# The last product of a two-MLP kernel: from part Strassen to Strassen for all k pairs, with tiles parked in DRAM

## Chip, core and metric

The kernel runs on one core of a Trainium2 chip. Its time is the device time of one execution in microseconds: a median of 524.71 us over three runs (524.4 to 524.81). Traces come from a further execution taken with the hardware profiler. TensorE (PE) multiplies matrices out of SBUF into PSUM; VectorE (DVE) and ScalarE (ACT) work element by element; SP only issues DMAs here. Each engine works off its own instructions in order and waits for the others at semaphores.

## What is computed

Attention with a sigmoid in place of the softmax (2 batches, 12 heads, 448 positions, 64 per head); then two MLPs on the 896 tokens of 768 features:

```python
scores = scale * q @ k.T - log(448)
x = sigmoid(scores) @ v                          # 896 x 768
xn = x / rms(x) * g
x = (silu(xn @ w_gate) * (xn @ w_val)) @ w_out   # 768 -> 1536 -> 768
h = x @ w_in                                     # 768 -> 2048
out = (h * sigmoid(h)) @ w_out2                  # 2048 -> 768
```

All data is float32. The change is in the very last product, of K = 2048 (16 k tiles of 128, so 8 k pairs) with an output of 768 x 896, which is three chunks of two 128-row tiles by two batches of 448 columns.

## The kernel before

**Products.** A float32 operand is split into a high part rounded to fp32r and a low part, the rest (`high` on ScalarE, `low` on VectorE). A product of two tiles is three matmuls of 448 columns (`PASSES`: high-high, high-low, low-high). Activations stay in SBUF with features on partitions; weights come from DRAM in slabs of up to six 128x128 tiles, in an integer form that ScalarE (`exponent`, `tail_act`) and VectorE (`merge`) turn into float32. The pieces that matmuls read, high and low of up to 384 columns, lie in a ring of nine (`RING`); slabs arrive in two buffers (`raw`).

**Strassen.** A pair of k tiles, a pair of output tiles and the two batches form a 2x2 block product. Plainly (`weight_std`, `product`) that is eight tile products. `weight_mac` and `group` do it in seven, in Winograd's form: weights A11, A12, A22 and the sums S1 to S4 (four VectorE operations more), activations B11, B21, B22 and T1 to T4. `ORDER_OF` is the order of the seven groups; one group runs over all k pairs in turn. What must be added between the results is saved from PSUM by ScalarE (`save`) and added by VectorE; TensorE adds further products into the same bank once that bank is saved.

**Activations for Strassen.** `formed` makes all seven from a float32 tile of a k pair (on VectorE seven operations of 448 columns and two of 896, on ScalarE three and two) and needs 3.5 tiles of [128, 2, 2, 448]; `halved` only splits (2 tiles); `late` makes the T's of a halved pair with the 640-column tile `spare` as its only room (14 VectorE and 4 ScalarE operations of 448 columns). The input product's outputs g2_0 to g2_7 are such float32 tiles. There are 23.5 tiles in all: `whole` lists free ones, `part` free halves, `reserve` how many wholes others must leave.

**The last product before.** Chunk 0 (e0) takes k pairs 0 to 3 by Strassen and 4 to 7 plainly, chunk 1 (e1) 0 to 4 and 5 to 7, both by `mixed` with the plain part first. Chunk 2 (e2, `phased`) takes pairs 0 to 2 by Strassen, pair 7 plainly, then pairs 3 to 6. Pairs 0 and 1 are formed during the input product; 2 and 3 when its last tile has begun; 4 to 7 are halved, and `late` turns 4, 5 and 6.

**Order.** `Plan` holds all this work as jobs with costs and dependencies. Matmuls have a fixed order; `Plan.run` gives each job of VectorE (D), ScalarE (A) and SP (S) a due time counted back from its users and places it by list scheduling over fixed costs (`LAG`, line 37: a DMA takes 0.4 us of SP and lands 4.4 us later). The instructions are issued in the order so found. SP issues all weight loads (line 237) and all output stores (line 1382).

Of the kernel before, what the change touches and what calls it, by code (L numbers as in the profile page):

```python
# [34 lines left out]
IDLE = 9  # L35
SQUARED = 10
# [15 lines left out]
RESERVE = 6  # L52
# [143 lines left out]
def tile_attention_two_mlps(  # L196
# [378 lines left out]
    ep = ctx.enter_context(tc.tile_pool(name="ep", bufs=1, reuse_waits="tile"))  # L575
    pools = {"T": tp, "F": fp, "x": xp, "r": rp, "e": ep}
# [16 lines left out]
    whole, part, reserve = [], {}, [0]  # L593
# [178 lines left out]
    ORDER_OF = ("A11", "S1", "S2", "A12", "S3", "S4", "A22")  # L772
    USES = dict(zip(ORDER_OF, ("B11", "T1", "T2", "B21", "T3", "B22", "T4")))

# [175 lines left out]
    def phased(name, phases, slab, keys, book, fdep, put, own):  # L950
# [3 lines left out]
        single = {a: Banks(f"{name}{a}") for a in ("A11", "S1", "S2", "S3")}  # L954
        where = dict(single, A12=ba.bank(0), S4=ba.bank(1), A22=bb.bank(0))
        bw = bb.bank(1)
        opens = dict(single, A12=ba, A22=bb)
        saved, e = {}, {}
# [8 lines left out]
        def add(j, src, other, deps):  # L967
            def go():
                if j not in saved:
                    saved[j] = saved_tile(name, j)  # L970
                tt(saved[j], src(), saved[other], ALU.add)

            return dve(S, go, deps)

        def save(j, src, dep):
            def go():
                saved[j] = saved_tile(name, j)
                nc.scalar.activation(saved[j], src(), AF.Copy)

            return scalar(S, go, [dep, sdone[j]], psum=True)  # L980

        list(groups(0))
        w = [6 * slab + i for i in range(2 * len(keys))]
        n = len(keys)
        product([where["A12"], where["S4"]], w[:n], keys, (0, 1), first=False, final=False)
        product([where["A22"], bw], w[n:], keys, (1,), last=False)
        p2 = product([where["A22"], bw], w[n:], keys, (0,), first=False, final=False)
        w1 = save(3, bw, p2[-1])
        for n in range(1, len(phases) - 1):
            list(groups(n))  # L990
        for a, g in groups(len(phases) - 1):
            if a == "A11":
                v0 = save(0, where[a], g)
                single[a].read_by(v0)
            elif a == "S1":
                v1 = save(1, where[a], g)
                single[a].read_by(v1)
# [67 lines left out]
    def late(key, q, deps, free, book, fdep, own):  # L1065

        (h11, l11), (h12, l12), (h21, l21), (h22, l22) = [
            [lambda m=m, j=j, b=b: act[key, 2 * q + m](j, b) for j in range(2)] for m in range(2) for b in range(2)
        ]
        t = spare[:, :S]  # L1070
        last = list(deps)

        def op(a, b, what, **more):
            get = lambda v: t if v is None else v().bitcast(F32)
            last[:] = [dve(S, lambda: tt(t, get(a), get(b), what), list(last), **more)]
            return last[0]

        def parted(name, to=None, deps=()):
            def hi_():
                if to:  # L1080
                    book[name] = tuple(v() for v in to)
                else:
                    h = half(f"{key}{q}{name}")
                    book[name] = (h[1][:, 0], h[1][:, 1])
                    own[name] = [h]
                high(book[name][0], t)

            h = scalar(S, hi_, last + list(deps), need=None if to else some)
            last[:] = [dve(S, lambda: low(book[name][1], t, book[name][0]), [h])]
            fdep[name] = list(last)  # L1090

        def plain_ones():
            for name, p in (("B11", (h11, l11)), ("B21", (h21, l21)), ("B22", (h22, l22))):
                book[name] = tuple(v() for v in p)

        begin = op(h12, h11, ALU.subtract, take="alt")
        begin.then(plain_ones)
        for name in ("B11", "B21", "B22"):
            fdep[name] = [begin]
        op(None, l12, ALU.add)  # L1100
        op(None, l11, ALU.subtract)
        parted("T1")
        op(h22, None, ALU.subtract)
        op(None, l22, ALU.add)
        parted("T2")
        op(None, h11, ALU.subtract)
        op(None, l11, ALU.subtract)
        parted("T3")
        op(h21, lambda: book["T2"][0], ALU.subtract)
        op(None, lambda: book["T2"][1], ALU.subtract)  # L1110
        op(None, l21, ALU.add)
        parted("T4", (h12, l12), [free])
        plan.frees("alt", last[0])

    def formed(key, q, tile_, deps, book, fdep, own, gate=None):
# [27 lines left out]
        ls = split(f"{key}{q}t", srcs, [[t1, t3], [t2, t4]], keep, lambda: tile_.back(int(q < 2)))  # L1143
# [20 lines left out]
    class Whole:  # L1164
# [96 lines left out]
    for p in range(1, NP1):  # L1261
# [7 lines left out]
        if p in (1, 2):  # L1269
            formed("h", p - 1, f[p - 1], fdone[p - 1], hbook[p - 1], hdep[p - 1], hown[p - 1])  # L1270
# [63 lines left out]
    def over():  # L1334
        give_all(hrest)
        reserve[0] = RESERVE

# [5 lines left out]
    gbook, gdep, gown, grest = [{} for q in range(5)], [{} for q in range(5)], [{} for q in range(4)], []  # L1343
# [156 lines left out]
```

## Time and profile before

| | us |
|---|---|
| median of three timed runs | 524.71 |
| span of the profiled execution | 527.0 |
| TensorE busy | 522.6 |
| VectorE busy | 467.4 |
| ScalarE busy | 378.3 |
| DMA, mean over the span | 122 GB/s |

The page gives no time of the profiled execution beside its span, first to last instruction. A busy time is what an engine spent in instructions. Matmuls are pipelined and overlap in the trace, so their number and the distance of their starts say more than the length of one.

### The profile page before, as it was taken

The numbers are of one execution on the slowest core, as the hardware profiler recorded it, in microseconds if no ns is written. First come the engines' busy times: TensorE is split into PE (matmuls) and PEld (weight loads), VectorE is DVE, ScalarE is ACT, GpSimd is POOL, SyncE is SP. The second block draws the span as 40 slices with busy tenths as digits, with TensorE's granted clock in tenths as the row PEclk, the third lists the DMA queues.
The fourth block names the chain that finished last, engine by engine and source line by source line (L and its number), as shares of the span: only waits on it lengthen the run. The fifth ranks groups of instructions, "written<-read, shape, count | busy, mean of one in ns | idle before, by whom it ended". The sixth has DMA issues, their size and how long they took to land.

```text
span 527.0 us, 7412 instructions
## 1 busy us (share of the span) xinstructions
PE 522.6 (99%) x2678; PEld 447.4 (85%) x2678; DVE 467.4 (89%) x855; ACT 378.3 (72%) x658; POOL 0.2 (0%) x4
## 2 busy tenths in 40 slices
PE   9999999999999999999999999999999999999997
PEld 4444469999999999999999999999899999999996
DVE  6799999999998979799989899998875999969984
ACT  6876754787877686857596688998887967565540
POOL 0000000000000000000000000000000000000000
PEclk9999999999999999999999999999999999999999
DMA  8764111033333343412533543422533214525201
GB/s 303 284 247 159 60 61 60 1 120 121 119 121 119 125 176 92 150 40 66 194 109 111 168 153 115 163 95 101 176 111 121 99 61 133 171 95 187 75 1 70
DMA packets 16292, 65.01 MB, mean 123 GB/s; under 512 B 2048, under 2 KB 4608, under 8 KB 16256
## 3 DMA queue, kind: packets, MB, share of 16 engines
q1 hardware_dynamic: 16112, 64.32, 35.4%
q8 instruction: 21, 0.34, 0.3%
q10 hardware_dynamic: 144, 0.23, 0.1%
q14 instruction: 15, 0.12, 0.1%
HBM read 61.79 MB, written 2.75 MB: 122 GB/s over the span
## 4 chain that ended last, share of the span: by engine, by line
PE 98%; DVE 1%; ACT 1%; issue 0%; ACTq 0%
PE sc L380 6%; PE av L407 6%; PE v L737 3%; PE e2S L786 2%; PE e1x L786 2%; PE g L737 2%; PE e0x L786 2%; PE e0b L737 2%; PE e0a L737 2%; PE o2x L786 2%; PE o1x L786 2%; PE o0x L786 2%; PE e2a L786 2%; PE i5x L786 1%; PE i4x L786 1%; PE e1b L737 1%
## 5 line engine op out<-in xcount | busy, mean ns | idle before, releaser
L267 DVE SCALAR_TENSOR_TENSOR f<-f,raw 128x768 uint32<-128x768 uint32 (+1 forms) x68 | 61.6, 907 | 9.1 <-ACT f L255 7.3
L263 ACT ACTIVATE raw<-raw 128x768 int32<-128x768 uint32 (+1 forms) x68 | 56.9, 841 | 15.8 <-DMA raw<-in_w 12.2
L255 ACT ACTIVATE f<-raw 128x768 f32<-128x768 f32 (+1 forms) x68 | 58.5, 862 | 7.2 <-DVE w_S L246 3.2
L243 ACT ACTIVATE w_S<-f 128x384 fp32r<-128x384 f32 (+1 forms) x82 | 40.8, 500 | 18.1 <-DVE f L695 6.4
L246 DVE TENSOR_TENSOR w_S<-f,w_S 128x384 fp32r<-128x384 f32 (+1 forms) x82 | 43.4, 531 | 8.4 <-ACT w_S L243 7.6
L389 ACT ACTIVATE a<-sc,logs 128x896 f32<-128x896 f32 x42 | 39.2, 1008 | 15.5 <-PE sc L380 15.5
L243 ACT ACTIVATE w_A<-f 128x384 fp32r<-128x384 f32 (+2 forms) x79 | 39.1, 503 | 12.6 <-PE o2y L737 1.8
L246 DVE TENSOR_TENSOR w_A<-f,w_A 128x384 fp32r<-128x384 f32 (+2 forms) x79 | 41.5, 536 | 4.8 <-ACT w_A L243 4.5
L407 PE MATMUL av<-a,vr 128*64 128x448 f32 (+1 forms) x192 | 35.4, 552 | 0.0
L407 PEld LDWEIGHTS av<-a,vr 128*64 128x64 f32 (+1 forms) x192 | 10.4, 135 | 21.3 <-issue 20.3
L380 PEld LDWEIGHTS sc<-ks 64*128 64x128 f32 x204 | 18.5, 188 | 10.7 <-issue 5.0
L380 PE MATMUL sc<-ks 64*128 64x448 f32 x204 | 25.2, 385 | 0.0
L246 DVE TENSOR_TENSOR w<-f,w 128x384 fp32r<-128x384 f32 (+1 forms) x34 | 15.7, 482 | 3.8 <-ACT w L243 3.6
L243 ACT ACTIVATE w<-f 128x384 fp32r<-128x384 f32 (+1 forms) x34 | 15.3, 464 | 5.2 <-PE o0x L786 1.1
L243 ACT ACTIVATE w_S<-s 128x384 fp32r<-128x384 f32 x24 | 12.5, 520 | 6.4 <-PE g L737 3.1
L737 PE MATMUL v<-x,w 128*128 128x448 f32 x72 | 15.3, 370 | 0.0
L737 PE MATMUL g<-x,w 128*128 128x448 f32 x72 | 15.3, 368 | 0.0
L737 PEld LDWEIGHTS g<-x,w 128*128 128x128 f32 x72 | 13.4, 188 | 1.7 <-issue 0.7
L737 PEld LDWEIGHTS v<-x,w 128*128 128x128 f32 x72 | 13.5, 188 | 1.4 <-issue 0.4
L702 DVE TENSOR_TENSOR f<-f 128x384 f32<-128x384 f32 (+2 forms) x27 | 14.3, 532 | 0.2
L246 DVE TENSOR_TENSOR w_S<-s,w_S 128x384 fp32r<-128x384 f32 x24 | 13.2, 552 | 0.9 <-ACT w_S L243 0.9
L246 DVE TENSOR_TENSOR ks<-kq,ks 128x896 fp32r<-128x896 f32 (+2 forms) x14 | 13.2, 949 | 0.4
(1461 smaller groups left out, 1489.0 us busy)
## 6 DMA issues: line engine op xcount, KB each, us to landing
raw<-in_w SPq DMA_DIRECT2D x56, 768.0 KB, 4.4
raw<-in_w SPq DMA_DIRECT2D x18, 512.0 KB, 3.6
kq<-in_kq SPq DMA_DIRECT2D x11, 448.0 KB, 5.4
vr<-in_v SPq DMA_DIRECT2D x6, 256.0 KB, 5.0
vr<-in_v SPq DMA_DIRECT2D x6, 192.0 KB, 2.5
out_t<-e0s SPq DMA_DIRECT2D x4, 224.0 KB, 3.0
out_t<-e1s SPq DMA_DIRECT2D x4, 224.0 KB, 2.2
out_t<-e2s SPq DMA_DIRECT2D x4, 224.0 KB, 1.9
```

The costliest lines, as they stand in the source:

```text
L243: nc.scalar.activation(dst, src, AF.Copy)
L246: nc.vector.tensor_tensor(dst, src, hi.bitcast(F32), ALU.subtract)
L255: nc.scalar.activation(floats[s], words(s)[:, :, 1].bitcast(F32), AF.Prelu, scale=2.0**-112, alpha=2.0**32)
L263: nc.scalar.activation(z.bitcast(I32), z, AF.Copy, scale=2.0**-29 * (1 - 2.0**-18), bias=-0.5 + 2.9e-5)
L267: nc.vector.scalar_tensor_tensor(fu, fu, 3, words(s)[:, :, 0], ALU.logical_shift_left, ALU.bitwise_or)
L380: nc.tensor.matmul(ps[to, h, :S], k_[:, keys], q_, start=(step == 0), stop=(step == 2 or plain), skip_group_check=True,)
L389: nc.scalar.activation(a, ps[:, :, :S], AF.Sigmoid, bias=logs, scale=D**-0.5)
L407: nc.tensor.matmul(av[n][h * D : (h + 1) * D, :S], vr[i][rows, c, h, :], a[rows, h, :], start=(begun[n] == 1), stop=(begun[n] == KC + 1), ...
L702: s4 = dve(hw, lambda: tt(block(1), block(1), block(0), ALU.subtract), [s2, l3])
L737: nc.tensor.matmul(banks[b](), t[:, jw], act[key](jx, b), start=(first and i == 0 and n_ == 0), stop=(final and i == n - 1 and n_ == 2), s ...
L786: nc.tensor.matmul(ps(), w[:, jw, j * P : (j + 1) * P], book[t][USES[a]][jx], start=(start and i == 0 and n == 0), stop=(stop and i == len ...
```

## The change

All eight k pairs of all three chunks go by Strassen.

Pairs 0, 1 and 2 are formed during the input product (`FIRST`). g2_3 to g2_6 are written to DRAM when they are done and brought back when a tile is free and the pair named in `AFTER` is through (`away`); then each is formed, as is pair 7. `halved` and `late` are no longer used for the last product.

Chunk 0 runs as e0 (pairs 0 to 3) and e0b (4 to 7), chunk 1 as e1 (0 to 4) and e1b (5 to 7). The first part (`half_sum` without `put`) leaves its sum in a float32 tile, which goes to DRAM; the second part (with `put`) gets it back, adds every result onto it, seven VectorE additions in place of three saves and three additions, and stores the output. The order is e0, e1, e2, e0b, e1b. Chunk 2 takes four phases of two pairs, its sums kept in PSUM, and gives back the tiles of each pair as it goes. Its weights come in slabs of four tiles. All new DMAs are issued by SP.

Cut to its core; left out are the deletion of `late`, changes of argument lists, the pool for DRAM tiles and the unchanged start of `phased`:

```diff
+FIRST = (0, 1, 2)
+AFTER = {3: 1, 4: 2, 5: 4, 6: 4, 7: 4}
+AWAY = (3, 4, 5, 6)
-RESERVE = 6
...
-    def phased(name, phases, slab, keys, book, fdep, put, own):
+    def half_sum(name, macs, book, fdep, to, put=None, deps=()):
+
+
+        bx, by, bz = (Banks(f"{name}{n}") for n in "xyz")
+        saved = {}
+
+        def save(j, src, dep):
+            def go():
+                saved[j] = saved_tile(name, j)
+                nc.scalar.activation(saved[j], src(), AF.Copy)
+
+            return scalar(S, go, [dep, sdone[j]], psum=True)
+
+        def add(m, b, src, j, deps):
+            def go():
+                d = to()[:, m, b]
+                tt(d, src(), d if put else saved[j], ALU.add)
+
+            return dve(S, go, deps, need=any_whole if not put and (m, b) == (0, 0) else None)
+
+        def first(m, b, j, src, dep):
+            return add(m, b, src, None, [dep, *deps]) if put else save(j, src, dep)
+
+        def done(m, b, dep):
+            if put:
+                put(m, b, lambda: to()[:, m, b], dep)
+            return dep
+
+        g = lambda ps, a, **k: group(macs, ps, a, book, fdep, **k)
+        g1 = g(bx, "A11", start=True, first=bx)
+        v0 = first(0, 0, 0, bx, g1)
+        g2_ = g(by, "S1", start=True, first=by)
+        v1 = first(1, 1, 1, by, g2_)
+        g3 = g(bx, "S2", deps=[v0])
+        v2 = first(0, 1, 2, bx, g3)
+        g4 = g(bz, "A12", start=True, stop=True, first=bz)
+        a00 = done(0, 0, add(0, 0, bz, 0, [g4, v0]))
+        bz.read_by(a00)
+        g5 = g(bx, "S3", deps=[v2])
+        a11 = done(1, 1, add(1, 1, bx, 1, [g5, v1, a00]))
+        g6 = g(by, "S4", stop=True, deps=[v1])
+        a01 = done(0, 1, add(0, 1, by, 2, [g6, v2, a00]))
+        by.read_by(v1, a01)
+        g7 = g(bx, "A22", stop=True, deps=[a11])
+        if put:
+            a10 = done(1, 0, add(1, 0, bx, None, [g7, *deps]))
+        else:
+            sdone[:3] = a00, a11, a01
+            a10 = scalar(S, lambda: nc.scalar.activation(to()[:, 1, 0], bx(), AF.Copy), [g7, a00], psum=True)
+        bx.read_by(a10)
+        return [a00, a11, a01, a10]
+
...
+    def phased(name, phases, book, fdep, put, own):
...
-
-        list(groups(0))
-        w = [6 * slab + i for i in range(2 * len(keys))]
-        n = len(keys)
-        product([where["A12"], where["S4"]], w[:n], keys, (0, 1), first=False, final=False)
-        product([where["A22"], bw], w[n:], keys, (1,), last=False)
-        p2 = product([where["A22"], bw], w[n:], keys, (0,), first=False, final=False)
-        w1 = save(3, bw, p2[-1])
-        for n in range(1, len(phases) - 1):
+            return dve(S, lambda: tt(at(j), src(), saved[other], ALU.add), [*deps, sdone[j]])
+
+        def result(m, b, src, j, deps):
+            r = dve(S, lambda: tt(at(j), src(), saved[j], ALU.add), deps)
+            put(m, b, lambda: at(j), r)
+            return r
+
+        for n in range(len(phases) - 1):
             list(groups(n))
...
             elif a == "S2":
-                u2 = add(2, where[a], 0, [g, v0, sdone[2]])
-                single[a].read_by(u2)
-                c01 = add(1, lambda: saved[2], 1, [u2, v1])
-                c11 = add(3, lambda: saved[1], 3, [c01, w1])
+                u2 = add(2, where[a], 0, [g, v0])
+                read_(a, u2)
+                c01 = add(3, lambda: saved[2], 1, [u2, v1])
             elif a == "A12":
-                a00 = add(0, where[a], 0, [g, u2])
-                put(0, 0, lambda: saved[0], a00)
+                a00 = result(0, 0, where[a], 0, [g, u2])
+                read_(a, a00)
             elif a == "S3":
                 u3 = add(2, where[a], 2, [g, c01])
-                a11 = add(3, where[a], 3, [g, c11])
-                single[a].read_by(u3, a11)
-                put(1, 1, lambda: saved[3], a11)
+                read_(a, u3)
+                a11 = result(1, 1, lambda: saved[2], 1, [u3])
             elif a == "S4":
-                a01 = add(1, where[a], 1, [g, c11])
-                ba.read_by(a00, a01)
-                put(0, 1, lambda: saved[1], a01)
+                a01 = result(0, 1, where[a], 3, [g, c01])
+                read_(a, a01)
             else:
-                a10 = add(2, where[a], 2, [g, u3])
-                bb.read_by(w1, a10)
-                put(1, 0, lambda: saved[2], a10)
+                a10 = result(1, 0, where[a], 2, [g, a11])
+                read_(a, a10)
+        ba.read_by(*[j for a in two[:2] for j in ends[a]])
+        bb.read_by(*ends[two[2]])
+        sdone[:] = a00, a11, a10, a01
...
             if self.got[1] is None:
                 self.got = full(self.name)
-                reserve[0] = max(reserve[0] - 1, 0)
+                reserve[0] = max(reserve[0] - 1, least[0])
             return self.got[1]
 
...
+        def away(self, deps):
+            home = dram.tile([P, 2, 2, S], F32, name=f"{self.name}away")
+
+            def bring():
+                self.got = full(self.name)
+                nc.sync.dma_start(self.got[1], home)
+
+            def left():
+                whole.append(self.got[0])
+                self.got = None, None
+
+            go = plan.add("S", 0.4, lambda: nc.sync.dma_start(home, self.got[1]), deps).then(left)
+            return go, lambda need: plan.add("S", 0.4, bring, [go], need=lambda: len(whole) > reserve[0] and need())
...
-        reserve[0] = RESERVE
+        reserve[0] = least[0] = 1
...
-    settled = lambda: some() and g2[-1].got[1] is not None
+    bring = {}
...
-        if p in (0, 1):
+        if p in FIRST:
             formed("g", p, g2[p], gdone[p], gbook[p], gdep[p], gown[p])
-    for q in range(4, NP2):
-        halved("g", q, g2[q], gdone[q], grest, settled)
-    for q in (2, 3):
-        formed("g", q, g2[q], gdone[q], gbook[q], gdep[q], gown[q], (lambda: settled() and g2[2].given) if q == 3 else settled)
+        if p in AWAY:
+            bring[p] = g2[p].away(gdone[p])[1]
+    begun7 = []
+    gdone[NP2 - 1][0].then(lambda: begun7.append(1))
+    held = [Whole(f"e{p}") for p in range(2)]
+    settled = lambda: some() and begun7
+
+    def lower():
+        least[0] = 0
+        reserve[0] = 0
+
+    for q in range(len(FIRST), NP2):
+        after = lambda q=q: g2[AFTER[q]].given
+        deps = [bring[q](after)] if q in AWAY else gdone[q]
+        gate = lambda after=after, ready=some if q == len(FIRST) else settled: ready() and after()
+        formed("g", q, g2[q], deps, gbook[q], gdep[q], gown[q], gate)
...
-    for p in range(2):
-        wide_ = 1 + p
-        keys = [("g", k) for k in range(6 + 2 * wide_, K2)]
-        macs = [(s + 3, 3), (s + 5, 1)] if p == 0 else [(s + 2, 3), (s + 4, 2)]
-        for j, tiles in enumerate((6, 6, 4) if p == 0 else (6, 6)):
-            weight_std(s + j, ZE, tiles)
-        weight_mac(macs, ZE)
-        macs = [(macs[0][0], range(3)), (macs[1][0], range(3, 3 + wide_))]
-        mixed(f"e{p}", macs, s, keys, gbook, gdep, put(p))
-        for q in (4,) if p == 0 else (5, 6):
-            late("g", q, parts_of(q), read["g", 2 * q], gbook[q], gdep[q], gown[q])
-        s += 6
+    weight_mac([(s, 3), (s + 2, 1)], ZE)
+    h0 = half_sum("e0", [(s, range(3)), (s + 2, (3,))], gbook, gdep, held[0])
+    bring.update(e0=held[0].away(h0)[1])
+    s += 3
+    weight_mac([(s, 3), (s + 2, 2)], ZE)
+    h1 = half_sum("e1", [(s, range(3)), (s + 2, (3, 4))], gbook, gdep, held[1])
+    bring.update(e1=held[1].away(h1)[1])
+    s += 4
+    plan.pe[-1].then(lower)
+    for n in range(4):
+        weight_mac([(s + 2 * n, 2)], ZE)
+    phased("e2", [[(s + q, (q, q + 1))] for q in range(0, NP2, 2)], gbook, gdep, put(2), gown)
+    s += 8
+    weight_mac([(s, 3), (s + 2, 1)], ZE)
+    half_sum("e0b", [(s, (4, 5, 6)), (s + 2, (7,))], gbook, gdep, held[0], put(0), [bring["e0"](lambda: g2[-1].given)])
+    s += 3
     weight_mac([(s, 3)], ZE)
-    weight_std(s + 4, ZE, 4)
-    weight_mac([(s + 2, 3), (s + 5, 1)], ZE, False)
-    phases = [[(s, range(3))], [(s + 2, range(3, 6)), (s + 5, (6,))]]
-    phased("e2", phases, s + 4, [("g", 14), ("g", 15)], gbook, gdep, put(2), gown)
+    half_sum("e1b", [(s, (5, 6, 7))], gbook, gdep, held[1], put(1), [bring["e1"](lambda: g2[-1].given)])
...
-    output("moe2_w_out", K2, (2, 4, 8), 6)
+    t = _slabs(inputs["moe2_w_out"], K2)
+    for k0, m, ns in ((0, 0, (6, 2)), (0, 2, (6, 4)), (0, 4, (4, 4, 4, 4)), (8, 0, (6, 2)), (10, 2, (6,))):
+        for n in ns:
+            if n == 2:
+                slab(t[m : m + 2, k0 : k0 + 2].reshape(-1, P, P))
+            else:
+                strassen(t[m : m + 2, k0 : k0 + n])
+            k0 += n
```

## Rows read from the trace of the kernel before

**Rows 1.** The profile page, part 1: engine, busy us and share of the span, instructions
```profile
PE 522.6 (99%) x2678; PEld 447.4 (85%) x2678; DVE 467.4 (89%) x855; ACT 378.3 (72%) x658; POOL 0.2 (0%) x4
```
**Rows 2.** The page, part 4: the chain that ended last, share by engine
```profile
PE 98%; DVE 1%; ACT 1%; issue 0%; ACTq 0%
```
**Rows 3.** Waits of weight loads, 130 to 527 us: total us, times, longest
```profile
PEld i5x L786 <- ACT i5s L818: 0.4, 1, 0.4
PEld i4x L786 <- ACT i4s L818: 0.3, 1, 0.3
```
**Rows 4.** The chain in order of time: start us, us, engine, tile, line, instructions
```profile
375.15 1.82 PE i5x L786 x9
378.82 2.12 PE i5x L786 x9
380.94 1.86 PE i5z L786 x9
...
521.06 2.49 PE e2b L786 x12
```
**Rows 5.** Busy us by window, input product and last product; then clock, DMA share, GB/s
```profile
310.00:414.20 104.20, 104.17 (x510) 95.29 (x509) 89.10 (x155) 89.37 (x155) 0.00 (x0) 1.00 0.38 131
414.20:523.60 109.40, 109.34 (x530) 98.97 (x528) 95.57 (x184) 63.12 (x121) 0.00 (x0) 1.00 0.28 94
```
**Rows 6.** Timeline of the last matmul and what follows: start us, us, engine
```profile
523.17 0.37 PE L786 MATMUL e2b<-x1h,w_A 128*128 128x448 f32 x1
523.58 0.62 DVE L971 TENSOR_TENSOR e2s<-e2b,e2s 128x448 f32<-128x448 f32 x1 [1.85 <-PE e2b L786]
```
**Rows 7.** VectorE by line and shape, 310 to 527 us: busy us, mean ns
```profile
L267 DVE SCALAR_TENSOR_TENSOR f<-f,raw 128x768 uint32<-128x768 uint32 x24 | 22.8, 954 | 4.3 <-ACT f L255 3.9 <-ACT raw L263 0.2
L246 DVE TENSOR_TENSOR w_S<-f,w_S 128x384 fp32r<-128x384 f32 x33 | 18.3, 554 | 3.3 <-ACT w_S L243 2.9
...
L1045 DVE TENSOR_TENSOR g<-g 128x448 f32<-128x448 f32 x16 | 9.8, 618 | 0.0
...
L267 DVE SCALAR_TENSOR_TENSOR f<-f,raw 128x512 uint32<-128x512 uint32 x4 | 2.7, 687 | 0.0
...
L246 DVE TENSOR_TENSOR w_S<-spare,w_S 128x128 fp32r<-128x128 f32 x4 | 1.1, 288 | 0.0
```
**Rows 8.** VectorE's timeline: instructions that follow one another directly
```profile
418.45 1.69 DVE L246 TENSOR_TENSOR g2B<-g,g2B 128x448 fp32r<-128x448 f32 x3
...
421.40 2.09 DVE L246 TENSOR_TENSOR g7l<-g,g7h 128x896 fp32r<-128x896 f32 x2
```
**Rows 9.** Windows, columns as in Rows 5: two dense stretches of VectorE
```profile
100.00:200.00 100.00, 100.00 (x495) 92.67 (x494) 92.56 (x167) 76.54 (x138) 0.00 (x0) 1.00 0.34 119
...
490.00:503.00 13.00, 13.00 (x65) 11.81 (x64) 12.79 (x28) 4.87 (x11) 0.00 (x0) 1.00 0.08 31
```
**Rows 10.** ScalarE's timeline: a save from PSUM, three casts of a block
```profile
403.73 0.53 ACT L818 ACTIVATE i7s<-i7x 128x448 f32<-128x448 f32 x1
...
415.41 1.51 ACT L243 ACTIVATE g2B<-g 128x448 fp32r<-128x448 f32 x3
```
**Rows 11.** DMA issues: count, KB each, median us from issue to landing
```profile
raw<-in_w SPq DMA_DIRECT2D x56, 768.0 KB, 4.4
raw<-in_w SPq DMA_DIRECT2D x18, 512.0 KB, 3.6
...
out_t<-e0s SPq DMA_DIRECT2D x4, 224.0 KB, 3.0
...
out_t<-e2s SPq DMA_DIRECT2D x4, 224.0 KB, 1.9
```
**Rows 12.** ScalarE's waits for DMA, 310 to 414 us: total us, times, longest
```profile
ACT raw L263 <- DMA raw<-in_w: 5.5, 6, 1.6
```
**Rows 13.** The weight loads of line 237: us to landing
```profile
DMA to landing us min/median/max: 3.4/4.4/7.8
```

More of the change, by code (lines that the diff above doesn't have):

```diff
@@ L575, in tile_attention_two_mlps @@
     ep = ctx.enter_context(tc.tile_pool(name="ep", bufs=1, reuse_waits="tile"))
+    dram = ctx.enter_context(tc.tile_pool(name="dram", bufs=1, space=bass.MemoryType.DRAM))
     pools = {"T": tp, "F": fp, "x": xp, "r": rp, "e": ep}
@@ L588, in tensor @@
         return plan.add("P", 0.2027 * n, fn, deps, **more)
-    whole, part, reserve = [], {}, [0]
+    whole, part, reserve, least = [], {}, [0], [0]
     def new(tag, dtype, name, n=2):
@@ L948, in mixed @@
         sdone[3] = put(1, 0, lambda: saved[3], a10)
-    def phased(name, phases, slab, keys, book, fdep, put, own):
-        ba, bb = Banks(f"{name}a", True), Banks(f"{name}b", True)
[L954 to L958, printed above, removed]
+    def half_sum(name, macs, book, fdep, to, put=None, deps=()):
[40 more added lines that the diff above has]
+        return [a00, a11, a01, a10]
@@ L960, in groups @@
+    def phased(name, phases, book, fdep, put, own):
+        ba, bb = Banks(f"{name}a", True), Banks(f"{name}b", True)
+        single = {a: Banks(f"{name}{a}") for a in SINGLE}
+        two = [a for a in ORDER_OF if a not in SINGLE]
+        where = dict(single, **{two[0]: ba.bank(0), two[1]: ba.bank(1), two[2]: bb.bank(0)})
+        opens = dict(single, **{two[0]: ba, two[2]: bb})
+        saved = {}
         def groups(n):
@@ L965, in groups, with at, save, read_ @@
                 )
-        def add(j, src, other, deps):
[L968 to L980, printed above, removed]
-        list(groups(0))
-        w = [6 * slab + i for i in range(2 * len(keys))]
-        n = len(keys)
-        product([where["A12"], where["S4"]], w[:n], keys, (0, 1), first=False, final=False)
-        product([where["A22"], bw], w[n:], keys, (1,), last=False)
-        p2 = product([where["A22"], bw], w[n:], keys, (0,), first=False, final=False)
-        w1 = save(3, bw, p2[-1])
-        for n in range(1, len(phases) - 1):
-            list(groups(n))
+        def at(j):
+            if j not in saved:
+                saved[j] = saved_tile(name, j)
+            return saved[j]
+        def save(j, src, dep):
+            return scalar(S, lambda: nc.scalar.activation(at(j), src(), AF.Copy), [dep, sdone[j]], psum=True)
+        def add(j, src, other, deps):
+            return dve(S, lambda: tt(at(j), src(), saved[other], ALU.add), [*deps, sdone[j]])
[4 more added lines that the diff above has]
+        for n in range(len(phases) - 1):
+            list(groups(n))
+        ends = {}
+        def read_(a, *jobs):
+            if a in single:
+                single[a].read_by(*jobs)
+            ends.setdefault(a, []).extend(jobs)
         for a, g in groups(len(phases) - 1):
@@ L1063, in halved, with formed @@
             adep[(key, 2 * q + m), 0] = adep[(key, 2 * q + m), 1] = [ls[m]]
[L1065 to L1115, printed above, removed]
+    def formed(key, q, tile_, deps, book, fdep, own, gate=None, keep_=0):
         blocks = [lambda m=m, b=b: tile_()[:, m, b] for m in range(2) for b in range(2)]
@@ L1142, in formed @@
         srcs = [lambda m=m: tile_()[:, m] for m in range(2)]
-        ls = split(f"{key}{q}t", srcs, [[t1, t3], [t2, t4]], keep, lambda: tile_.back(int(q < 2)))
+        ls = split(f"{key}{q}t", srcs, [[t1, t3], [t2, t4]], keep, lambda: tile_.back(keep_))
         fdep["T1"] = fdep["T3"] = [ls[0]]
@@ L1269, in tile_attention_two_mlps @@
         if p in (1, 2):
-            formed("h", p - 1, f[p - 1], fdone[p - 1], hbook[p - 1], hdep[p - 1], hown[p - 1])
+            formed("h", p - 1, f[p - 1], fdone[p - 1], hbook[p - 1], hdep[p - 1], hown[p - 1], keep_=1)
     for q in (2, 3):
@@ L1335, in over @@
         give_all(hrest)
-        reserve[0] = RESERVE
+        reserve[0] = least[0] = 1
     plan.pe[-1].then(over)
     NP2 = K2 // 2
-    gbook, gdep, gown, grest = [{} for q in range(5)], [{} for q in range(5)], [{} for q in range(4)], []
+    gbook, gdep, gown = [{} for q in range(8)], [{} for q in range(8)], [{} for q in range(8)]
     g2 = [Whole(f"g2_{p}") for p in range(NP2)]
     gdone = {}
-    settled = lambda: some() and g2[-1].got[1] is not None
+    bring = {}
     for p in range(NP2):
@@ L1455, in output @@
             strassen(pair[:, :6])
-            if mini == 8:
-                strassen(pair[:, 6:12])
-                plain(pair[:, 14:], False, 4)
-                slab(pair[:, 12:14].reshape(-1, P, P))
-                continue
             if mini == 2:
```

10 lines of the change are left out of this document (4 added, 6 removed).

## The prediction

> **What bounds the kernel now.** I read the page from the top: TensorE is busy 99% of the span and VectorE 89% [rows 1]; the chain of work that ended last is TensorE for 98% of its length [rows 2]. A busy row alone could hide a waiting engine, so next came the waits: from 130 us on TensorE's weight loads stood still twice, 0.4 and 0.3 us, both times for a ScalarE save [rows 3]. From 130 us to the last matmul the kernel is therefore a count of matmuls times an interval. The chain gives the interval [rows 4]: 9 matmuls in 1.82 us (0.2027 each) up to 378.8 us; then the group with the second of the two short waits, 2.12 us; after it 9 in 1.86 and at the very end 12 in 2.49 us (0.2067 each). The granted clock is 1.00, its upper level of 2.4 GHz, in the whole of both stages [rows 5], so the step of 2% is no clock gate; I don't know its cause. The last product runs from 414.2 to 523.6 us; 528 matmuls at 0.2067 are 109.1 us, which is the 109.4 of the window [rows 5]. Behind the last matmul come a hand-over of 0.4 us, one VectorE add of 0.62 and the last store, 3.4 us to the end of the span [rows 5, 6].
>
> **The change, part by part.**
>
> 1. *Matmuls.* A block of (k pair, output pair) is eight 128x448 products as it stands and seven by Strassen, each product three matmuls. Before, chunks 0, 1 and 2 take 4, 5 and 7 of their 8 pairs by Strassen: (28+32) + (35+24) + (49+8) = 176 products, 528 matmuls. After, all 24 blocks: 168 products, 504 matmuls. That removes 24, at 0.2067 us 4.96 us, at 0.2027 us 4.86 us. Since nothing stands between TensorE and the end, all of it comes off the path as long as the others keep up. I take 4.9. The Trainium skill, TensorE: Matmul & The Clock Gate, Back-to-back issue gap, puts the warm interval at columns/2.4 GHz plus 2.5 ns, 189 ns for 448 columns; the sum by it would be 4.5 us. The rows show 203 to 207 ns and decide.
>
> 2. *VectorE work of the last product*, from which a new bound would come. Durations are those of [rows 7]; instructions that follow one another directly start 0.085 us closer than one lasts (three of 448 columns take 1.69 us, two of 896 take 2.09) [rows 8], so I count 0.535 us for 448 columns, 1.00 for 896, 0.467 for 384, 0.20 for 128, 0.335 (the middle of these two) for 256, and 0.87 and 0.60 for merging a slab of 768 and of 512. A Strassen weight set of 3 pairs (2 merges, 4 sums, 7 low parts) costs 6.88 us, of 2 pairs 4.90, of 1 pair 2.80; a plain slab of 6 tiles 1.80, of 4 tiles 1.27.
> Weights: before 4 x 6.88 + 4.90 + 2 x 2.80 + 4 x 1.80 + 2 x 1.27 = 47.8 us; after 4 x 6.88 + 5 x 4.90 + 2 x 2.80 = 57.6 us: plus 9.9.
> Activations: a pair made by `formed` costs 7 x 0.535 + 2 x 1.00 = 5.75 us, by `halved` 2.00, by `late` 14 x 0.535 = 7.49. Before, pairs 2 and 3 formed, 4 to 7 halved, 4 to 6 made late: 42.0 us; after, pairs 3 to 7 formed, 28.8: minus 13.2. (Pair 2 moves ahead, see 3.)
> Adds of the outputs: 6 + 6 + 8 = 20 before, 10 + 10 + 7 = 27 after: plus 3.7.
> Sum plus 0.4 us, in a stage that becomes 5 us shorter. It stood at 95.6 of 109.4 [rows 5]. About 6 us of pair 3 fall before the stage, and two halvings (2 us) no longer do, so I get 92 of 104 us, 89%. That is below what the trace already bears without a wait of TensorE: 92.6 of 100 in the window from 100 to 200 us and 12.8 of 13 from 490 to 503 [rows 9]. Cost nothing; bounds below.
>
> 3. *The stage before* (input product of the second MLP, 104.2 us). It gets pair 2's forming (9 VectorE instructions, 5 of ScalarE) and, since chunk 0 now begins with Strassen and reads pair 3 after the first nine matmuls (1.9 us into the stage), nearly all of pair 3's. VectorE stood at 89.1 [rows 5]; plus 2 x 5.75 minus 2.0 is 98.6 of 104.2, 95%. ScalarE, at 89.4, gains two formings (three casts of 448 columns take 1.51 us [rows 10], two of 896 by their columns some 2 more) and loses two to four casts for halving: under 95% too. Pair 3 must come back from DRAM and find 3.5 free tiles. With pairs 0 to 2 formed (10.5) and g2_7 the code has 13 until the last strassen of that stage gives back its operands group by group: seven groups of 1.86 us before 414.2, so 1.5 tiles at 403, after the first, and 3 at 410.5, after the fifth. Time enough, but little: this is where I expect the first short waits, of the 0.3 to 0.4 us of [rows 3]. I take one, 0.4 us; bounds nothing and 3 us (a forming of 5.75 us starting at 410.5 is through at 416.3, and T1 is wanted at 418.6; two instructions of others ahead in each step use that up).
>
> 4. *Parking.* Four tiles g2_3 to g2_6 and two half sums go to DRAM and back: 12 transfers of 896 KB, all on SP's queue with the weight loads. Loads of 512 and 768 KB land 3.6 and 4.4 us after issue, a store of 224 KB at 1.9 [rows 11]; the slopes put 896 KB at 4.8 to 5.0 us, an estimate from those rows, and the planner's own figures are 0.4 + 4.4. DMA is 38% busy in the input product and 28% in the last [rows 5]: 11 MB more is there. Stores wait on SP until ScalarE has written the tile, and weight loads stand behind them on that queue; a return waits until its store has landed. Both are planned seldom to be close. Cost taken: nothing, because the weight pieces are made up to nine ahead (8 x 1.86 us); the other end is a rival.
>
> 5. *Waits that are new.* In the second parts the first add on a bank is VectorE's, where ScalarE's save stood, and S2 waits for it: one group of 9 (1.86 us) or 12 (2.48) stands between, the add needs 0.4 + 0.62. Nothing if VectorE isn't behind; otherwise one weight piece (0.47) fits in too. Four such joints per chunk; bounds 0 and 8 x 0.5 = 4 us. The half sums must be home by the first add, 2.5 us into e0b; they are asked for once pair 7 is formed, some 5 us earlier at least. The tail is as before: last group, one add, one store.
>
> 6. *Where space binds.* 23.5 tiles hold pairs 0 to 4 (17.5), g2_7 and a half sum, then most of pair 5; pairs 6 and 7 can only be formed when chunk 2's first phase (453 to 462 us on the old clock) gives back pairs 0 and 1, and are wanted at its fourth (479 to 481). In those 26 to 28 us VectorE has 11.5 us of forming, 2 of pair 5, and 10.7 us of weights (the rest of phase 1, phase 2, the opening of phase 3): 24.2. It fits at about 90%. If all of pair 5 slips into it too, it is 28: then some 2 to 4 us are late. I take 0.
>
> Sum: the profiled execution's span is 527.0 us; minus 4.9 plus 0.4 is 522.5. The timed runs shown have a median of 524.71, 2.3 us less than that execution, and the same difference gives **520.2 us**.
>
> **The rivals.**
>
> *A. VectorE becomes the bound* in the two tight places, pair 3's forming (point 3) and the stretch before phase 3 (point 6). For it: 95% and 90% are averages, and space, not work, sets when it may start. Against it: the trace bears 98% over 13 us. Price 3 us, the mean of point 6's 2 to 4: 523.2, reaching 525.
>
> *B. The parked tiles hold up the weights: slower.* In the input product ScalarE already stood six times for a weight load that had just landed, up to 1.6 us [rows 12]: loads come just in time, and a load behind a parked tile comes later. The same 224 KB store took 3.0 us to land while loads ran (e0s) and 1.9 without (e2s) [rows 11]; the longest load took 7.8 against a median of 4.4 us [rows 13], so 3.4 us is what a queue has cost here. ScalarE, standing in its order for that load, holds the save that TensorE's next group but one needs; that save has 1.86 us less its own 0.53 [rows 10] and 0.4, some 0.9 us to spare, so a hit costs 2.5 us. Two of the 12 transfers hitting take back the gain; three make 524.71 - 4.9 + 7.5 = 527.3. Against it: TensorE never waited for DMA after 130 us [rows 3], though loads were waited for. The Trainium skill, DMA: Bandwidth & Descriptors, Queues, rings and completion order, says that each DMA engine consumes a ring's descriptors in order; by that rule a weight load can't pass a parked tile issued before it, which is this rival; the e0s and e2s rows agree with it.
>
> *C. The faster interval stays.* If neither short wait recurs and 0.2027 holds to the end, some 672 matmuls gain 0.004 each, 2.7 us: 517.5. For it: the step came right after the second wait. Against it: more waits are likelier than fewer, and the profiled execution is 2.3 us longer than the timed ones, so these may be without the step already.
>
> **How the numbers follow.** Forecast (519 to 521.5) 0.50; A 0.20; B 0.20; C 0.10. About 0.2%, 1.05 us, is what a measurement can tell from no change. Faster than 523.66: the forecast, C and half of A, 0.70. Within: 0.05 of A and 0.05 of B (two hits), 0.10. Slower: 0.15 of B and A at its worst, 0.05, together 0.20. The range reaches down to C and up past A into B, 517.5 to 526.5, leaving out some 0.05 below and 0.13 of B.
>
> **What would show it.** 504 matmuls from the first of e0 to the last, in about 104.2 us at 0.2067; TensorE without waits over 0.5 us; VectorE near 95% before the stage and 89% in it. A would show as TensorE waiting for g pairs 3 or 6 and 7, with VectorE unbroken before. B would show as ScalarE waiting on raw for over 3 us right behind a parked transfer, and TensorE on a save. The prediction is wrong if the stage shrinks by less than 4 us, or if the input product grows by more than 1.

## The result, and the profile after

The changed kernel takes 528.01 us (median of 5 runs, 527.41 to 528.61), the kernel before beside it 524.81 (524.4 to 525.63): a ratio of 1.0057, 95% interval 1.0045 to 1.007, slower by 0.57%. Forecast were 520.2 us. The profiled execution took 528.61, its span (first to last instruction) is 526.8 us; in every run below the time is 1.7 to 2.4 us above the span.

The page of the kernel after, part 1, then the shares of its chain by engine, answer [rows 1, 2]:

```profile
PE 518.7 (98%) x2654; PEld 444.0 (84%) x2654; DVE 470.2 (89%) x882; ACT 381.0 (72%) x677; POOL 0.2 (0%) x4
...
PE 76%; DVE 10%; DMA 8%; ACT 3%; issue 2%; ACTq 0%; DVEq 0%
```

The 24 matmuls are gone (2678 to 2654). The chain (the work that ended last, followed back) is new: TensorE had 98% of it, now VectorE and DMA hold 18%. The waits of weight loads from 130 us on, the view of [rows 3], say where:

```profile
PEld i5x L791 <- DVE g L829: 2.5, 1, 2.5
PEld i6x L791 <- DVE g L829: 1.4, 1, 1.4
PEld e0y L791 <- DVE x2l L248: 0.7, 1, 0.7
PEld e0x L791 <- ACT e0s L964: 0.5, 1, 0.5
...
```

L829 is VectorE's add that finishes a block of the output of a Strassen group in the input product. The two largest waits stand there, in i5 and i6, a stage whose matmuls the change doesn't touch. What VectorE and ScalarE waited for, 340 to 527 us (total us, times, longest):

```profile
ACT raw L265 <- DMA raw<-in_w: 10.2, 7, 2.6
DVE g L829 <- DMA g_5away<-g: 3.7, 1, 3.7
DVE g L829 <- DMA g_4away<-g: 2.9, 1, 2.9
```

ScalarE's wait for weight loads is longer than in [rows 12] too: in the same window, 310 to 414 us, 7.7 us in 6 waits, the longest 2.6. The new thing is that VectorE's add waits for a *store*: that of g2_4 to DRAM holds up the first add of g2_5, that of g2_5 the first of g2_6. The DMAs, the view of [rows 11] (KB each, us from issue to landing), are far from the 4.8 to 5.0 us of the prediction, all but the first store, ahead of which no load had gone out for 12 us; the four returns take 7.6 to 9.3:

```profile
g_3away<-g SPq DMA_DIRECT2D x1, 896.0 KB, 3.8
g_4away<-g SPq DMA_DIRECT2D x1, 896.0 KB, 6.8
g_5away<-g SPq DMA_DIRECT2D x1, 896.0 KB, 8.2
g_6away<-g SPq DMA_DIRECT2D x1, 896.0 KB, 7.3
g<-g_3away SPq DMA_DIRECT2D x1, 896.0 KB, 7.8
...
g<-g_6away SPq DMA_DIRECT2D x1, 896.0 KB, 9.3
```

The timeline of the kernel after shows one such hit whole (start us, us, engine; the idle time before it and its releaser in brackets):

```profile
380.18 0.33 SPq L1202 DMA_DIRECT2D g_4away<-g  x1
...
387.03 0.62 DVE L829 TENSOR_TENSOR g<-i5z,i5s 128x448 f32<-128x448 f32 x1 [2.86 <-DMA g_4away<-g]
...
388.24 0.88 PE L791 MATMUL i5x<-y0h,w_A 128*128 128x448 f32 x3 [2.09 <-DVE g L829]
...
389.29 0.57 PE L791 MATMUL i5x<-x,w_A 128*128 128x448 f32 x1
389.66 0.57 PE L791 MATMUL i5x<-lone,w_A 128*128 128x448 f32 x1
```

The store is issued at 380.18 and lands at 387.0; the add runs at once; TensorE's next group starts 1.2 us after that, and then its matmuls start 0.37 us apart instead of 0.20. The windows of the kernel after, columns as in [rows 5], with the stretch of those slow matmuls last:

```profile
310.50:414.00 103.50, 100.34 (x485) 91.87 (x485) 90.47 (x164) 86.06 (x154) 0.00 (x0) 0.98 0.46 161
414.00:523.00 109.00, 108.48 (x529) 98.56 (x527) 96.68 (x201) 68.83 (x140) 0.00 (x0) 1.00 0.48 166
...
389.00:391.00 2.00, 2.00 (x7) 1.79 (x6) 1.09 (x3) 1.81 (x3) 0.00 (x0) 0.50 0.00 0
```

At 0.50 the granted clock is at 1.2 GHz, the lower of its two levels; TensorE had just stood for over 2 us. Added up over TensorE's starts from i0 on, against 0.2027 per matmul, the gaps are 3.9 us at i5 (2.25 of standing, the rest almost all matmuls at the lower level), 1.3 at i6, 1.0 in e0 (pair 3 formed late) and 0.6 in e0b; with the smaller ones 6.9.

### The profile page after: what moved, and what is told of

It is laid out like the page before. It is cut to its first block, busy times and chain, and to the rows that moved or that the text cites. A ratio compares the mean times of both kernels' runs of the same rounds, so it can differ in the third digit from the quotient of the medians.

```text
span 526.8 us, 7458 instructions
## 1 busy us (share of the span) xinstructions
PE 518.7 (98%) x2654; PEld 444.0 (84%) x2654; DVE 470.2 (89%) x882; ACT 381.0 (72%) x677; POOL 0.2 (0%) x4
## 4 chain that ended last, share of the span: by engine, by line
PE 76%; DVE 10%; DMA 8%; ACT 3%; issue 2%; ACTq 0%; DVEq 0%
DMA raw<-in_w 7%; PE av L409 7%; PE sc L382 6%; PE g L740 3%; PE v L740 3%; PE e1x L791 2%; PE o2x L791 2%; PE o1x L791 2%; PE o0x L791 2%; DMA g_5away<-g 2%; DVE f L269 1%; PE e0x L791 1%; PE e1bx L791 1%; PE g4x L791 1%; PE g2x L791 1%
## 5 line engine op out<-in xcount | busy, mean ns | idle before, releaser
L269 DVE SCALAR_TENSOR_TENSOR f<-f,raw 128x768 uint32<-128x768 uint32 (+1 forms) x65 | 58.3, 900 | 6.3 <-ACT f L257 5.0
L257 ACT ACTIVATE f<-raw 128x768 f32<-128x768 f32 (+1 forms) x65 | 55.6, 859 | 7.9 <-DVE w_S L248 4.6
L245 ACT ACTIVATE w_S<-f 128x384 fp32r<-128x384 f32 (+1 forms) x90 | 44.6, 496 | 21.9 <-DVE f L698 9.6
L248 DVE TENSOR_TENSOR w_S<-f,w_S 128x384 fp32r<-128x384 f32 (+1 forms) x90 | 47.1, 526 | 6.6 <-ACT w_S L245 6.1
L245 ACT ACTIVATE w_A<-f 128x384 fp32r<-128x384 f32 (+1 forms) x84 | 41.3, 501 | 9.2 <-PE o2y L740 1.8
L248 DVE TENSOR_TENSOR w_A<-f,w_A 128x384 fp32r<-128x384 f32 (+1 forms) x84 | 43.8, 534 | 2.6 <-ACT w_A L245 2.4
L1102 DVE TENSOR_TENSOR g<-g 128x448 f32<-128x448 f32 x32 | 19.8, 620 | 0.1
L705 DVE TENSOR_TENSOR f<-f 128x384 f32<-128x384 f32 (+1 forms) x30 | 15.8, 526 | 0.2
L245 ACT ACTIVATE w_A<-spare 128x128 fp32r<-128x128 f32 (+1 forms) x21 | 7.0, 335 | 10.0 <-DVE spare L269 8.0
L687 DVE TENSOR_TENSOR s<-f 128x384 f32<-128x384 f32 x24 | 13.3, 554 | 0.3
```

Of the source, the lines that this page charges most:

```text
L245: nc.scalar.activation(dst, src, AF.Copy)
L248: nc.vector.tensor_tensor(dst, src, hi.bitcast(F32), ALU.subtract)
L257: nc.scalar.activation(floats[s], words(s)[:, :, 1].bitcast(F32), AF.Prelu, scale=2.0**-112, alpha=2.0**32)
L269: nc.vector.scalar_tensor_tensor(fu, fu, 3, words(s)[:, :, 0], ALU.logical_shift_left, ALU.bitwise_or)
L705: s4 = dve(hw, lambda: tt(block(1), block(1), block(0), ALU.subtract), [s2, l3])
L1102: sub = lambda d, a, b: (lambda: tt(d(), a(), b(), ALU.subtract))
```

## The experiments

*Parked* is a tile that is written to DRAM to come back later; *room* is a free tile in SBUF. The theory after the first look was *room*: VectorE's first add into a new output tile has to wait until a parked one has left. Its rivals: *queue* (a weight load behind a parked tile reaches ScalarE late, rival B of the prediction), *issue* (SP's queue is what delays the stores) and *the profile before* (the trace that the prediction rests on wasn't an ordinary one).

**The kernel before once more.** No edit.

> The kernel before, unchanged, with a new trace. What is asked is the interval of the matmuls and the span of an ordinary execution. If the interval of 0.2027 us holds to the end unless a wait of TensorE changes it, the span should be some 523 us (the timed 524.7 less the 1.8 us that lie between time and span after the change), and the 527.0 of the profile shown carried some 4 us of its own. If 0.2067 in the last product belongs to the program, the span is 526 to 527 again and the times stay at 524.7.

524.99 us (524.45 to 525.67, 10 runs), ratio 0.9982 [0.9956, 1.0008]; span 522.9. From 130 us on TensorE waits for nothing, and at the very end, where [rows 4] have 12 in 2.49, the chain of this execution has:

```profile
516.97 2.45 PE e2b L786 x12
```

The ten runs have spans of 522.7 to 523.9, so 0.203 is the ordinary interval of the kernel before, and the trace that the prediction read was of an execution with a span 4.1 us longer. Beside it the kernel after reads: from the first matmul of i0 to the end of the span 213.4 us before (522.9 - 309.48), 216.3 after (526.8 - 310.52). That is minus 4.9 for 24 matmuls, plus 6.9 for the gaps; the 0.9 left is nearly all matmuls at 0.2067 instead of 0.2027, some 200 of them behind the waits in i6 and e0b. The rest of the difference in span, 1.0 us, lies ahead of i0, in stages that the change doesn't touch and that differ from run to run.

**Room: pair 2 formed later.** A gate lets pair 2 begin only when pair 1 has given back its float32 tile.

```diff
-            formed("g", p, g2[p], gdone[p], gbook[p], gdep[p], gown[p])
+            gate = (lambda: some() and g2[1].given) if p == 2 else None
+            formed("g", p, g2[p], gdone[p], gbook[p], gdep[p], gown[p], gate)
```

> The changed kernel, with one edit: pair 2 may take room only when pair 1 has given back its float32 tile. Theory (room): pairs 0, 1 and 2 take their rooms at once, each stays one half short and keeps its float32 tile, so a single tile rotates among g2_4, g2_5 and g2_6 and VectorE must wait for the store of one before it writes the next (2.9 and 3.7 us, TensorE 2.3 and 1.2 of them, and a lower clock for some 1.2 us). Then these waits go, and the time falls by 4 to 5 us, to 523 to 524, or below to 520 if the rest of the sum holds. Rival (queue: the weight loads come late behind parked tiles, whatever the room): the stores are still there and in the same queue, so 527 to 528 stays within 1 us.

523.97 us (522.59 to 527.24, 12 runs), ratio 0.9968 [0.994, 0.9997]. In this kernel room of pairs 4 to 7 that chunk 2 gives back is taken again while e0b and e1b still read it, so a part of their products has other values. Waits of VectorE for a store are gone, and the time falls by 4.0 us. A new wait of TensorE stands in i6 (waits of weight loads from 130 us on, of ScalarE from 340 us on; the trace is of the run of 526.24 us):

```profile
PEld i6x L791 <- ACT i6s L823: 2.3, 1, 2.3
...
ACT raw L265 <- DMA raw<-in_w: 8.2, 6, 3.1
```

Its timeline is rival B: a load issued right behind the store of g2_4, landed 7.8 us later, ScalarE standing for it, and the save of i6x behind that in ScalarE's order:

```profile
379.15 0.33 SPq L1202 DMA_DIRECT2D g_4away<-g  x1
379.57 12.66 SPq L239 DMA_DIRECT2D raw<-in_w  x3
...
387.41 0.90 ACT L265 ACTIVATE raw<-raw 128x768 int32<-128x768 uint32 x1 [3.12 <-DMA raw<-in_w]
...
391.94 0.53 ACT L823 ACTIVATE i6s<-i6x 128x448 f32<-128x448 f32 x1
```

So both theories hold, one behind the other: *room* was the first limit, and *queue* the next.

**The same gate, and chunk 2 gives back the room of pairs 0 to 3 only:**

```diff
-... gbook, gdep, put(2), gown)
+... gbook, gdep, put(2), gown[:4] + [{}] * 4)
```

> The changed kernel with pair 2 gated as in gate_pair2, and with chunk 2 giving back only pairs 0 to 3. Same order up to the last product. The save behind a weight load that is late should cost TensorE some 2 us in the input product again, and the time be 523 to 524.5, as in gate_pair2; if gate_pair2's 523.97 came from reading wrong room early, it would move by more than 1 us.

524.02 us (522.44 to 527.65, 10 runs), ratio 0.9974 [0.9954, 0.9994]; one wait of note, 2.0 us at the same save of i6x. So what chunk 2 gives back isn't where the time is. The trace is of the run of 522.44 us, with the granted clock at 1.00 behind that wait; five of the ten runs have a mean granted clock of 0.996 or 0.997, about what the runs traced with a stretch at 0.50 have, so the median holds more than the wait.

**A quarter of the bytes stored**, in the changed kernel and in the one with the gate and the kept room. The return, not shown, becomes four DMAs of 224 KB:

```diff
-go = plan.add("S", 0.4, lambda: nc.sync.dma_start(home, self.got[1]), deps).then(left)
+n = S if self.name[0] == "e" else S // 4
+store = lambda: nc.sync.dma_start(home[:, :, :, :n], self.got[1][:, :, :, :n])
+go = plan.add("S", 0.4, store, deps).then(left)
```

> The changed kernel with stores of a quarter of the bytes for g2_3 to g2_6 (the return fills the tile with that quarter four times, as many bytes as before; so what the product reads of these pairs is not the right data, and left out is the storing of three quarters). Room still rotates through one tile. If the length of the store while VectorE waits for its room is the cause, the waits on g_4away and g_5away shrink from 2.9 and 3.7 us to under 0.5 and the time falls by 3 to 5 us. If the return trips or the weight loads behind them cost it, it stays at 527 to 528.

524.16 us (523.25 to 526.88, 10 runs), ratio 0.9967 [0.9937, 0.9996]. The time falls by 3.9 us, as *room* has it. Of the two waits of VectorE for a store one is left, against the expectation (1.9 us, for that of g2_5), because even 224 KB took 5.5 us to land there; TensorE waits 0.6 us at i6 and no longer at i5. Its DMAs, columns as above:

```profile
g_4away<-g SPq DMA_DIRECT2D x1, 224.0 KB, 4.4
g_5away<-g SPq DMA_DIRECT2D x1, 224.0 KB, 5.5
g_6away<-g SPq DMA_DIRECT2D x1, 224.0 KB, 6.2
```

> gate2_kept with stores of a quarter of the bytes for g2_3 to g2_6 (the return fills the tile with that quarter four times; left out is the storing of three quarters). Order and room are those of gate2_kept. If late weight loads behind parked tiles are what is left of the loss, 2 MB less in the input product bring them in time: no wait of TensorE over 0.7 us there, and 520.5 to 522. If the loads are late for another reason, 523 to 524.5 stays.

521.91 us (521.15 to 522.06, 4 runs), ratio 0.993 [0.9916, 0.9943]. The save of i6x waits 0.2 us where it waited 2.0 with whole stores, and the median falls by 2.1 (the spans of the two traces by 1.4): with the gate on, the bytes in front of the weight load are the price.

**Issue: the four stores from ScalarE's queue.**

```diff
-go = plan.add("S", 0.4, lambda: nc.sync.dma_start(home, self.got[1]), deps).then(left)
+queue = nc.sync if self.name[0] == "e" else nc.scalar
+go = plan.add("S", 0.4, lambda: queue.dma_start(home, self.got[1]), deps).then(left)
```

> The changed kernel with the four stores of g2 tiles issued by ScalarE instead of SP, in the same order otherwise. If the stores are slow because they stand behind a weight load in SP's own ring (6.8 and 8.2 us against 3.8 for the one that met no load), they land in 4 to 5.5 us and the waits of VectorE shrink by 1.5 to 3 us each, the time by 2 to 4. If all DMAs share the same engines and the bytes in flight set the time, they still take 6 us or more and the time stays within 1 us of 528; ScalarE's issue of 0.4 us each adds nothing that can be seen.

528.6 us (526.29 to 532.67, 10 runs), ratio 1.0053 [1.002, 1.0086]: no better than the change itself. The stores take as long (DMAs, then the longer of VectorE's two waits for a store, 340 to 527 us; that for the store of g2_5 falls from 3.7 to 1.3, that for g2_4 rises from 2.9):

```profile
g_3away<-g ACTq DMA_DIRECT2D x1, 896.0 KB, 4.1
g_4away<-g ACTq DMA_DIRECT2D x1, 896.0 KB, 7.5
```

```profile
DVE g L829 <- DMA g_4away<-g: 3.7, 1, 3.7
```

That is what the Trainium skill, DMA: Bandwidth & Descriptors, Issuing engines are not separate DMA queues, says: transfers started by different engines run on the same 16 DMA engines and interleave. 7.5 and 7.8 us here against 6.8 and 8.2 from SP agree with it. So *issue* is not the cause.

**Gate, and a plan that knows the DMAs share a lane.** `Plan.run` lets every DMA land 4.4 us after its issue, however many stand before it. Here each adds its own length to one lane (0.0038 us per KB, 2.9 us for a slab of 768, 3.4 for a tile; that is 269 GB/s, what the gated kernel moved from 392.6 to 396 us at a DMA share of 0.90), so that loads and parked tiles are placed apart, and instructions that need them later (`kb` is set for weight loads and parked tiles, not shown):

```diff
+                    if j.kb:
+                        lane = max(lane, now + j.cost) + 0.0038 * j.kb
+                        end = max(end, lane + 1.3)
...
+            gate = (lambda p=p: some() and g2[p - 1].given) if p in (2,) else None
...
+... put(2), gown[:4] + [{}] * 4)
```

> The changed kernel with three edits: pair 2 takes room only after pair 1 has given back its float32 tile; the planner puts all loads and parked tiles through one lane of 3.8 ns per KB before it counts them as landed, so that instructions which need them are placed later; chunk 2 gives back only the tiles of pairs 0 to 3. Theory (two causes in a row: room, then loads that land late because parked tiles stand ahead of them): both are gone, no wait of TensorE over 0.5 us, the 24 matmuls come off at 0.2027 us each, 520 to 521 us. Rival (the bytes in flight themselves, or VectorE's load, cost it): 523 to 525, with waits in the input product again.

**520.82 us** (520.2 to 521.12, 5 runs; the kernel before beside it 525.55), ratio 0.9908 [0.9895, 0.9922]: faster than both kernels. TensorE waits for nothing from 130 us on; of waits for DMA, 340 to 527 us, ScalarE's two for a weight load are left, 1.0 us together (0.3 in the window of [rows 12]). The stores:

```profile
g_4away<-g SPq DMA_DIRECT2D x1, 896.0 KB, 7.9
g_5away<-g SPq DMA_DIRECT2D x1, 896.0 KB, 7.9
g_6away<-g SPq DMA_DIRECT2D x1, 896.0 KB, 8.1
```

The stores are no faster than in the changed kernel. After that of g2_4 the next load goes out 3.5 us later, where it was 1.0 (after) and 0.4 (with the gate alone):

```profile
376.46 0.42 SPq L1209 DMA_DIRECT2D g_4away<-g  x1
379.96 8.86 SPq L244 DMA_DIRECT2D raw<-in_w  x2
```

That load takes 6.2 us and lands at 386.2, only 1.4 us earlier than its like with the gate and the kept room (387.6). What changed more is ScalarE's order: it reads the slab behind the save of i6x now, 4.9 us after the landing, where it stood 2.8 us for it ahead of the save:

```profile
389.79 0.55 ACT L830 ACTIVATE i6s<-i6x 128x448 f32<-128x448 f32 x1 [0.26 <-PE i6x L798]
...
391.06 0.90 ACT L270 ACTIVATE raw<-raw 128x768 int32<-128x768 uint32 x1
```

From the first matmul of i0 to the end of the span it is 519.1 - 310.56 = 208.5 us, 4.9 less than the kernel before: 24 matmuls at 0.2027.

**The lane without the gate, and the lane in the kernel before.** The same lane and the same kept room with `formed(...)` as in the changed kernel; and the lane alone put into the kernel before.

> mended without the gate on pair 2: the planner knows how late DMAs land, but pairs 0 to 2 still keep their three float32 tiles while each lacks one half. If the room is a cause of its own, the planner can only place the wait, not remove it: waits of TensorE or of VectorE for a parked tile's room in the input product stay, several us in all, and the time is 525 to 530. If only the late loads cost, it is 520 to 521.5, as mended.

526.9 us (524.25 to 527.62, 10 runs), ratio 1.0022 [1.0001, 1.0043]. Against the expectation the input product has no wait of TensorE left (VectorE waits 0.8 us for a store); it went elsewhere (weight loads' waits from 130 us on, then a return of a tile):

```profile
PEld e0x L798 <- ACT lone L250: 1.2, 1, 1.2
PEld e0y L798 <- DVE g3th L253: 1.2, 1, 1.2
PEld e0y L798 <- ACT g3th L250: 1.1, 1, 1.1
```

```profile
g<-g_3away SPq DMA_DIRECT2D x1, 896.0 KB, 10.8
```

Without room, g2_3 is asked back only at 403.3 us (372.0 in the mended kernel), comes home at 414.1, and pair 3's forming, wanted at once by e0, stops TensorE instead: 5.7 us of gaps in all.

> The kernel before with the planner's lane of 3.8 ns per KB and nothing else. If what mended gained over the kernel before is the 24 matmuls and not a better order everywhere, this is 524.5 to 527, not faster than the kernel before. If the lane alone improves the order, it is 521 to 523.

526.39 us (525.85 to 527.8, 10 runs), ratio 1.0016 [1.0, 1.0032]. So what the mended kernel gains is not the lane's alone. Ratios to the kernel before: the change 1.0057, with the gate 0.9974, with the lane 1.0022, with both 0.9908 (these three with the kept room); the lane without the change 1.0016.

## Why the prediction was wrong

*Step that failed: part 4, "Cost taken: nothing, because the weight pieces are made up to nine ahead".* In the input product, for which parts 3 and 4 together took 0.4 us, the gaps were 5.3. Three things were missed. First, the pieces ahead don't cover a late *room*: the add into g2_5 stands in VectorE's order and can't be made ahead. Second, they don't cover a late load either where ScalarE stands for it with a save behind: with the gate on that cost TensorE 2.0 to 2.3 us, as rival B had it. Third, the landing was estimated at 4.8 to 5.0 us; three of the four stores and all four returns took 6.8 to 9.3.

*Part 3 laid the ground for it*, by its count of tiles: "with pairs 0 to 2 formed (10.5) and g2_7 the code has 13". Pairs 0 to 2 were not formed through. The last step of a pair, its two low parts of 896 columns, shows when it gives back its float32 tile. VectorE's timeline after, all such instructions from 343 to 420 us:

```profile
350.07 1.08 DVE L248 TENSOR_TENSOR g0tl<-g,g0th 128x896 fp32r<-128x896 f32 x1
...
364.24 1.09 DVE L248 TENSOR_TENSOR g1tl<-g,g0tl 128x896 fp32r<-128x896 f32 x1
...
369.92 1.09 DVE L248 TENSOR_TENSOR g2th<-g,g1tl 128x896 fp32r<-128x896 f32 x1
...
407.86 1.09 DVE L248 TENSOR_TENSOR h3tl<-g,g0th 128x896 fp32r<-128x896 f32 x1
410.20 1.09 DVE L248 TENSOR_TENSOR y<-g,g2B 128x896 fp32r<-128x896 f32 x1
...
411.61 1.09 DVE L248 TENSOR_TENSOR x<-g,g2th 128x896 fp32r<-128x896 f32 x1
```

One each at 350, 364 and 370, and the second of each only at 408 to 412, when the last strassen gives back its operands. For 38 us three pairs each hold a float32 tile and six of seven halves: 3 x (1 + 3) = 12 of the 13 tiles. One tile is left, and g2_3, g2_4, g2_5 and g2_6 go through it in turn, so each store's landing is on VectorE's path, and behind it TensorE's. With the gate, in the mended kernel:

```profile
350.10 1.08 DVE L253 TENSOR_TENSOR g0tl<-g,g0th 128x896 fp32r<-128x896 f32 x1
...
355.79 1.08 DVE L253 TENSOR_TENSOR g1th<-g,g0tl 128x896 fp32r<-128x896 f32 x1
...
359.90 1.08 DVE L253 TENSOR_TENSOR g0tl<-g,g0th 128x896 fp32r<-128x896 f32 x1
...
362.84 1.09 DVE L253 TENSOR_TENSOR g0tl<-g,g1th 128x896 fp32r<-128x896 f32 x1
```

Pairs 0 and 1 are through at 364, and their two float32 tiles are free.

*The others.* Part 1 was right: 4.9 us, which the mended kernel shows in full. Part 2 and the utilisation of part 3 too; the mended kernel's windows have VectorE at 94% in the input product (95 forecast) and 92.2 of 105.9 us, 87%, in the last (89 forecast), with no wait of TensorE in either (columns as in [rows 5]):

```profile
310.50:414.00 103.50, 103.50 (x513) 95.93 (x512) 97.48 (x175) 90.77 (x164) 0.00 (x0) 1.00 0.51 173
413.00:518.90 105.90, 102.61 (x507) 94.77 (x505) 92.19 (x191) 64.25 (x132) 0.00 (x0) 1.00 0.47 163
```

Pair 3's forming cost 1.0 us after, where part 3 took 0.4 and bounded it by 3. Part 5 at nothing held: no wait at the joints of the second parts, in the mended kernel or the changed one, whose 0.6 us of gaps in e0b were waits for weight pieces. Part 6 held: no wait of TensorE in chunk 2 of the changed kernel.

*The rivals.* B, with a chance of 0.20, had the right side, slower, and its mechanism shows as written once room is mended. In the changed kernel itself the larger part was the room, which no rival named; B's price of 2.5 us per hit was near for the wait (2.0 to 2.3 with the gate) but left out what the lower clock added in the trace of the kernel with the gate alone (3.8 us of gaps in all). A was wrong: VectorE was at 90 of 103.5 us in the input product and stood idle for a store. C's interval, 0.2027 to the end, was in fact the usual one: the trace of before was 4.1 us of span longer than another execution. The 2.3 us that the prediction took off its sum set a span against a time; what it comes to is the timed median less 4.5, and so its 520.2 stands near the 520.82 of the kernel in which TensorE waits for nothing.

What stays open: why TensorE's interval goes from 0.2027 to 0.2067 at one short wait and back at another; and why the granted clock fell after some waits of about 2 us and not after others.

## What to carry to other kernels

Count a pool's tiles by who still holds a source at that moment, not by what each job holds when it is done: several items begun together can each keep their last piece of room, and a buffer that only one tile rotates through puts every transfer's landing on the path. A transfer costs what stands in front of it. A plan that gives each a fixed landing time will place what reads it too early, and on an engine that works in order a wait for it holds up everything behind; planning with the lane took 3.2 us off the kernel with gate and kept room, of the 4.7 us that the mended kernel gains over the one before. Room and order both had to be mended: against the changed kernel, each by its ratio to the kernel before, the gate took 0.8%, the lane 0.35% and the two together 1.5%.

## What the runs showed of the hardware that was not expected

- How long a store took went with what was in flight when it was issued. Of the 24 stores of a whole g2 tile (896 KB) in six traces, the five issued with no weight load in flight (issued and not yet landed) landed after 3.8 to 4.3 us, the eleven with one in flight after 4.7 to 7.9, the eight with two after 7.3 to 9.1, from SP's queue or ScalarE's alike. A store of 224 KB, 1.9 us at the end of the kernel, took 2.9 to 3.0 with no load in flight and 3.4 to 6.2 with one or two: much of that time isn't its bytes.
- After a wait of 2.5 us, ahead of which the clock had been granted in full, TensorE's matmuls started 0.37 us apart at a granted clock of 0.50 (1.2 GHz) from 389.0 to 392.3 us; that cost 1.7 us more at i5. After 1.4 us in the same kernel, and after 2.0 in the trace with the gate and the kept room, the clock stayed; after 2.3 with the gate alone it fell, and after three waits of 1.2, 1.2 and 1.1 us close together with the lane and no gate too. The ten runs with the gate and the kept room differ among themselves (mean granted clock 1.00 in five, 0.996 to 0.997 in five), so these traces give no price for a wait of a given length.
